# Order of the first loads, of one batch's transposes and of one PSUM bank in a fused attention and FFN kernel

## The chip, the cores and the metric

The kernel runs on one core of one Trainium2 chip. The metric is the time of one execution on the device, in microseconds; less is better.

## The reference

There are 8 batches, 12 heads, 448 tokens and 64 elements per head. First comes attention with a squared relu in place of softmax, then a normalized FFN with a residual:

```python
scores = (1 / sqrt(64)) * q @ k.T                  # (8, 12, 448, 448)
attn   = max(scores, 0)**2 / 448
x      = (attn @ v), heads side by side            # (8, 448, 768)
xn     = (x - mean(x)) / sqrt(var(x) + 1e-6) * g_ln
out    = x + max(xn @ w_ch1, 0) @ w_ch2            # w_ch1 768 x 3072, w_ch2 3072 x 768
```

Inputs and output are float32 in HBM. The kernel computes in bfloat16 with float32 sums.

## The kernel before

Two heads make a pair, so there are 6 pairs per batch and pairs are numbered on through the batches: pairs 0 to 5 are batch 0, 6 to 11 batch 1, pair 12 begins batch 2. All the program's engine queues are written out by hand: within `tc.manual_schedule` each engine executes its instructions in the order in which the Python code emits them. What an engine waits for is added by the framework from the tiles that an instruction reads and writes.

**Three kinds of DMA queue.** GpSimd (POOL) issues nearly all loads, since they cast float32 to bfloat16 on the way. SyncE (SP) issues the DMA transposes and the stores. ScalarE (ACT) issues one load at the start and half of the last stores. On each of POOL and SP a DMA also waits until the one that used its semaphore before, eight DMAs earlier, has landed.

**The start.** `load_heads` (lines 145 to 163) emits POOL's loads of q, k and v of batches 0 and 1 from a list of pieces, `(name, first head, number of heads)`. "k" loads the first 384 keys of each head and "k last" the other 64; "v last" is four small loads. `load_early` (190 to 202) brings heads 0 and 1, which are pair 0, on another way: q by SP and k by ACT, in float32 into space that is free at that time, and three casts on VectorE and ScalarE make them bfloat16. It also loads the gains `g_sb`. `make_identity` writes the 128 x 128 identity on POOL with a memset and an affine select; TensorE needs it for the transposes of q and k in batches 0 and 1 (`pe_T`, line 236).

Meanwhile TensorE runs 15 matmuls on zeros (`warm_up`, line 714). Then `att_T(0)` transposes pair 0, and `step_fine` (772) goes through pairs 0 to 5: QK (line 301, or 296 for the last 64 keys of two pairs), relu on ScalarE (311), square on VectorE (314), AV (331). `att_T(2)` comes within pair 1, `att_T(3)` and `att_T(4)` follow.

**Each batch** then has FFN1 (`ffn_1_all`) and FFN2. FFN1 makes 24 column tiles of h, one per `ni`, with 12 matmuls each (447) and a relu on ScalarE (449). At certain `ni` (`IN_SECOND` for batch 1: 3, 6, 9, 13, 15, 18, 21) an `excursion` puts in three QK pieces of the next batch's attention. When the last QK of a pair is emitted, `queued` emits the transpose of the pair three later, `att_T` at line 260, on SP, and the loads of the pair six later are put on a list for POOL. Pairs from 12 on are transposed by DMA from `qk_ring`, which has three places. Three tiles `qkT` hold the transposed pairs in turn, so pair 15's transpose waits until TensorE has read pair 12's.

**x in token order.** Attention leaves x transposed, in `xT`. `ffn_x(b, ki)` (line 424) is a DMA transpose on SP that puts one sixth of it into `x_tok`; it is read for the statistics (`ffn_stats`, three VectorE instructions, lines 438 to 440, at the `ni` of `STATS_AT`) and for the residual. In batch 1 all six are emitted in batch 0's FFN2 (`ffn_2_first`), ahead of pair 15's transpose, which is emitted at `ni` 6 of batch 1's FFN1.

**FFN2 of batches 1 to 7** (`ffn_2_all`, `seven`) works on pairs of token tiles, with seven products in place of eight. A product is 24 matmuls (522) into one of three PSUM banks c, d, a. There are four single banks: `f_turn.items` (here f0 and f1) and `spare` (f2 and f3). Batch 7's FFN1 ends with three `unit`s, which also make seven products (673) in place of eight, in all four banks. The last unit has c = spare[0], d = f1, a = f0 and e = spare[1]. Its bank c is read by lines 688 (ScalarE) and 689 (VectorE), its bank e by line 700. FFN2 of batch 7 then begins with a product in `z_bank`, which is spare[0]. The very last product is cut in two, 256 and 128 columns; the 128 columns go to spare[1].

Of the kernel before, what the change touches and what calls it, by code (L numbers as in the profile page):

```python
# [11 lines left out]
def kernel(  # L12
# [10 lines left out]
    nc = tc.nc  # L23
# [6 lines left out]
    B, H, S, D = q.shape  # L30
# [33 lines left out]
    ps_pool = ctx.enter_context(tc.tile_pool(name="ps", bufs=1, space=bass.MemoryType.PSUM))  # L64

    identity = const_pool.tile([P, P], bf16)
    make_identity(nc, identity)
    eps_sb = const_pool.tile([P, 1], fp32)
    nc.vector.memset(eps_sb, 1e-6)
    first_sqrt = const_pool.tile([P, 1], fp32)  # L70
# [462 lines left out]
    def seven(b, pair, banks, last, between):  # L533

        m1, m2 = 2 * pair, 2 * pair + 1
        a11, a12 = (h[:, r, h_cols(b, m1)] for r in (slice(0, KH), slice(KH, K2)))
        a21, a22 = (h[:, r, h_cols(b, m2)] for r in (slice(0, KH), slice(KH, K2)))
        c, d, a = (bk[:, :HD] for bk in banks)
        bb = c
        acc1, acc2 = new_acc(), new_acc()  # L540
        tt = nc.vector.tensor_tensor
        sums = {}

        def after3():
            nc.scalar.copy(acc1, c)

        def after4():
            tt(acc1, d, acc1, op=Alu.add)

        def after1():  # L550
            tt(acc2, a, acc1, op=Alu.add)

        def finish(o_t, y, m, dh):
            nc.scalar.activation(o_t, y, Act.Identity, scale=rstd[:, m:m + 1])  # L554
            nc.gpsimd.tensor_tensor(o_t, o_t, x_half(m, dh), op=Alu.add)  # L555
            store(o_t, m, dh * HD, (dh + 1) * HD)

        def after5():
            tt(acc1, acc1, c, op=Alu.subtract)  # L559
            finish(new_o(), c, m1, 1)  # L560
            before7()

        def after2():
            tt(acc2, acc2, d, op=Alu.subtract)
            if last:
                scaled_plus(acc2, acc2, m2, x_half(m2, 1))
            finish(new_o(), d, m2, 0)

        def before7():
            if last:  # L570
                scaled_plus(acc1, acc1, m1, x_half(m1, 0))

        def after7():
            if last:
                scaled_plus(acc1, a, m1, acc1)
                store(acc1, m1, 0, HD)
                return
            tt(acc1, a, acc1, op=Alu.add)
            finish(acc1, acc1, m1, 0)

        def after6():
            tt(acc2, bb, acc2, op=Alu.add)
            finish(acc2, acc2, m2, 1)

        def s(name, x, y, op):
            def run():
                sums[name] = sum_of(x, y, op)
            return run

        steps = [  # L590
            (lambda: product(c, a11, B12, True), s(1, a11, a22, Alu.add), after3),
            (lambda: product(d, a22, B21, True), s(5, a11, a12, Alu.add), after4),
            (lambda: product(a, sums[1], B_SUM, True), s(2, a21, a22, Alu.add), after1),
            (lambda: product(c, sums[5], B22, False), s(7, a12, a22, Alu.subtract), after5),
            (lambda: product(d, sums[2], B11, False), s(6, a21, a11, Alu.subtract), after2),
            (lambda: product(a, sums[7], B_BOT, False), None, after7),
        ]
        if not last:
            steps.append((lambda: product(bb, sums[6], B_TOP, True), None, after6))
        for n, (mm, pre, post) in enumerate(steps):  # L600
            mm()
            flush()
            if pre:
                pre()
            posts.append(post)
            between(n)
        if last:
            cut = HD - P
            parts = ((bb, 0, cut), (spare[1], cut, HD))
            for ps, d0, d1 in parts:  # L610
                product(ps, sums[6], B_TOP, True, d0, d1)
                flush()

                def after(ps=ps, d0=d0, d1=d1):
                    o_t = acc2[:, d0:d1]
                    scaled_plus(o_t, ps[:, :d1 - d0], m2, o_t)
                    store(o_t, m2, HD + d0, HD + d1, (nc.sync, nc.scalar))
                posts.append(after)
            flush()
# [227 lines left out]
    T_IN_FIRST = {10: 3, 13: 4, 16: 5}  # L847
    X_AT = (9, 10, 11, 12, 13, 14)
    V_AT = {22: PE_T * NPAIR + 2, 23: PE_T * NPAIR + 4}
    STATS_AT = {0: (18, 21, 23), 1: (10, 16, 19, 22), 2: (2, 5, 8, 14), 3: (2, 5, 8, 11)}  # L850
    IN_SECOND = (3, 6, 9, 13, 15, 18, 21)
    IN_REST = (1, 3, 6, 9, 12, 15, 18)
    X_SUMS_AT = {0: (0, 1, 2), 4: (3,), 7: (4,)}
# [1 line left out]
    def ffn_1_all(b):  # L855
        ms = tiles_of(b)
        units = () if b < UNIT_FROM else (UNIT,) if b < B - 1 else (*LAST_UNITS, UNIT)
        for ni in range(NI0 if b == 0 else 0, units[0] if units else K2):
            if b == 0 and ni == NI0:
                ffn_1_first()  # L860
            if b == 0 and ni == NI0 + 2:
                x_carry(0)
            if b == 0 and ni == X_AT[0]:

                nc.sync.dma_start(held, h[:1, ni - 1, CARRY:CARRY + 16])
            if b == 0 and ni in X_AT:
                ffn_x(b, X_AT.index(ni))
            if b == 0 and ni == IN_FIRST[-1] + 1:
                flush_loads()
            if b == 0 and ni in V_AT:  # L870
                load_v(V_AT[ni])
            bursts = (IN_FIRST, IN_SECOND, IN_REST)[min(b, 2)]

            late = ni == 0 and b > 1 and b * S // (2 * P) - (b - 1) * S // (2 * P) == 1
            ffn_1(ni, spare[1] if late or b < B - 1 and ni in bursts and len(ready) > 1 else None)
            flush()
            at = STATS_AT[min(b, 2) if b < B - 1 else 3][:len(ms)]
            if ni in at:
                ffn_stats(ms[at.index(ni)])
            if b >= UNIT_FROM:  # L880
                for n in X_SUMS_AT.get(ni, ()):
                    x_sum(n)
            if b == 1:
                for n, part in enumerate(p for p, at in zip(LATE_SUMS, SUMS_AT) if at == ni):
                    if ni == REST_AT and n < 2:
                        ffn_2_first_rest(n)
                    w2_sums(*part)
            if b == 0:
                if ni in IN_FIRST:
                    excursion(3)  # L890
                if ni == IN_FIRST[-1] + 3:
                    next_AV(bank=spare[1])
                if ni in T_IN_FIRST:
                    att_T(NPAIR + T_IN_FIRST[ni])
            elif b < B - 1:
                if ni in bursts:
                    first = nc.vector if b > 1 and ni == bursts[0] else nc.scalar
                    excursion(3, third=(first, nc.vector), **(dict(evac_by=nc.scalar) if b == 1 else {}))
                    while ni > bursts[1] and held_stores:
                        held_stores.pop(0)()  # L900
                if b == 1 and ni == K2 - 1:
                    flush_loads()
                    next_AV(bank=spare[1])

        late = []

        def between(n):
            if n == 2:
                flush_loads()
            if n == 3:  # L910
                next_AV(bank=sc_turn.items[0][:, 0], evac_by=nc.scalar, later=late)
            if n == 5:
                posts.extend(late)


        f0, f1 = f_turn.items
        if b == B - 1:
            unit(units[0], (f0, spare[1], spare[0], f1), accs[0], accs[2])
            unit(units[1], (f1, f0, spare[1], spare[0]), accs[3], accs[4])
            unit(units[2], (spare[0], f1, f0, spare[1]), accs[0], accs[2])  # L920
        elif units:
            unit(UNIT, (f0, spare[1], spare[0], f1), accs[0], accs[1], between)

    CENTER_AT = (4, 6, 8)

    REST_AT = 3
    SUMS_AT = (1, 2, 3, 3, 3, 4, 7, 11)
    LATE_SUMS = [(o, x, y, op, part)
                 for o, x, y, op in ((B_SUM, B11, B22, Alu.add), (B_BOT, B21, B22, Alu.add),
# [2 lines left out]
    def ffn_2_first():  # L932
        b = 0
# [5 lines left out]
        for dh in range(2):  # L939
            for m, part in [(m, part) for m in range(2) for part in range(2 if dh else 4)]:  # L940
# [5 lines left out]
                if n in CENTER_AT:  # L946
                    steps[CENTER_AT.index(n)]()
                if n == 2:
                    for ki in range(K1):
                        ffn_x(1, ki)  # L950
                if n == 8:
                    carry(b)
# [13 lines left out]
    def ffn_2_all(b):  # L966
# [2 lines left out]
        z_bank = spare[0]  # L969
        first = b * S // (2 * P)  # L970
        pairs = range(first, (b + 1) * S // (2 * P))
        banks = [z_bank, y_bank, x_bank] if b == B - 1 else [y_bank, z_bank, x_bank]
        todo = []
        if b < B - 1:
            assert not ready
# [27 lines left out]
    ENGINES = [E.PE, E.Pool, E.DVE, E.Activation, E.SP]  # L1003

    with tc.manual_schedule(engines=set(ENGINES)):
        load_heads(0, [("q", 2, 2), ("k", 2, 2), ("k last", 0, 4), ("q", 4, 4), ("k", 4, 4),
                       ("k last", 4, 4), ("v", 0, 4), ("v last", 0, H), ("q", 8, 4), ("k", 8, 4),
                       ("k last", 8, 4), ("v", 4, 4), ("v", 8, 4)])
        load_early()
        load_heads(1, [("q", 0, 2), ("k", 0, 2), ("k last", 0, H)])  # L1010
        load_heads(1, [("q", 2, 4), ("k", 2, 4)])
        load_w1(0)
# [58 lines left out]
```

## Time and profile before

| | |
|---|---|
| Median of 4 runs | 518.27 us (517.08 to 520.14) |
| The profiled execution | 517.88 us, span 516.0 us |
| TensorE matmuls | 509.6 us busy, 99% of the span |
| VectorE | 402.6 us, 78% |
| ScalarE | 287.5 us, 56% |
| POOL | 223.9 us, 43% |
| HBM | 51.91 MB read, 11.01 MB written |

The span goes from the first to the last instruction of the core. Times in the views are from its start, in us. "Landing" is the time at which the semaphore of a DMA has reached its full count; the DMA list gives it as time since the issue. Matmuls overlap, so a busy TensorE is not one at its peak, and the step from one matmul's start to the next one's tells more of a wait than the idle time does. In a timeline, brackets after a row give the engine's idle time before it and what ended it.

### The profile page before, as it was taken

The numbers are of one execution on the slowest core, as the hardware profiler recorded it, in microseconds if no ns is written. First come the engines' busy times: TensorE is split into PE (matmuls) and PEld (weight loads), VectorE is DVE, ScalarE is ACT, GpSimd is POOL, SyncE is SP. The second block draws the span as 40 slices with busy tenths as digits, with TensorE's granted clock in tenths as the row PEclk, the third lists the DMA queues.
The fourth block names the chain that finished last, engine by engine and source line by source line (L and its number), as shares of the span: only waits on it lengthen the run. The fifth ranks groups of instructions, "written<-read, shape, count | busy, mean of one in ns | idle before, by whom it ended". The sixth has DMA issues, their size and how long they took to land.

```text
span 516.0 us, 14345 instructions
## 1 busy us (share of the span) xinstructions
PE 509.6 (99%) x5974; PEld 325.5 (63%) x5974; DVE 402.6 (78%) x720; ACT 287.5 (56%) x487; POOL 223.9 (43%) x257
## 2 busy tenths in 40 slices
PE   8999999999999999999999999999999999999996
PEld 4445567547875576655766557655766557667986
DVE  4966779968988689687885869987896869993855
ACT  5986642786248762487624876487624875234220
POOL 9727114888433853237632385346632000330031
PEclk9999999999999999999999999999999999999999
DMA  9999999999537992479924799369925300240022
GB/s 134 185 198 201 182 204 164 145 194 124 79 80 115 116 93 63 108 85 121 97 61 105 76 135 133 72 81 110 95 65 107 63 1 3 72 114 1 3 61 64
DMA packets 175280, 53.05 MB, mean 103 GB/s; under 512 B 154224, under 2 KB 175216, under 8 KB 175216
## 3 DMA queue, kind: packets, MB, share of 16 engines
q0 software_dynamic: 103712, 25.75, 55.2%
q1 hardware_dynamic: 70976, 26.03, 27.4%
q8 instruction: 46, 0.75, 0.7%
q10 hardware_dynamic: 528, 0.37, 0.2%
q14 instruction: 18, 0.15, 0.1%
HBM read 51.91 MB, written 11.01 MB: 122 GB/s over the span
## 4 chain that ended last, share of the span: by engine, by line
PE 93%; DVE 3%; DMA 2%; ACT 1%; issue 0%
PE f L522 34%; PE f L447 34%; PE f L673 6%; PE f L331 5%; PE sc L301 4%; PE f L501 3%; PE f L301 2%; DMA qkT_t<-qk_ring 2%; DVE at L314 2%; PE sc L296 1%; ACT at L311 1%; PE f L354 1%; PE sc L331 1%; PE f L236 1%; PE f L836 1%; DMA h<-in_q_dram 1%
## 5 line engine op out<-in xcount | busy, mean ns | idle before, releaser
L447 PE MATMUL f<-xc,w 128*64 128x448 bf16 x1872 | 189.0, 354 | 0.1
L447 PEld LDWEIGHTS <-w 128*64 128x64 bf16 x1872 | 105.1, 110 | 76.8 <-issue 14.5
L522 PE MATMUL f<-w,s_sb 128*64 128x384 bf16 (+2 forms) x1584 | 130.1, 324 | 0.0
L449 ACT ACTIVATE h<-f 128x448 bf16<-128x448 f32 x156 | 85.9, 551 | 65.1 <-PE f L447 60.1
L522 PEld LDWEIGHTS <-s_sb 128*64 128x64 bf16 x1584 | 95.4, 110 | 31.8
L311 ACT ACTIVATE at<-sc 128x896 bf16<-128x896 f32 x120 | 102.9, 918 | 9.3 <-PE sc L301 9.0
L314 DVE TENSOR_TENSOR at<-at 128x896 bf16<-128x896 bf16 x168 | 96.3, 619 | 7.1 <-ACT at L311 6.2
L555 POOL TENSOR_TENSOR o_t<-o_t,x_tok 128x384 f32<-128x384 f32 x26 | 25.3, 972 | 153.2 <-ACT o_t L554 153.2
L175 POOL DMA_DIRECT2D qk_ring<-in_q_dram x36 | 47.2, 1312 | 81.0 <-DMA qkT_t<-qk_ring 56.6
L554 ACT ACTIVATE o_t<-f,rstd 128x384 f32<-128x384 f32 x26 | 15.1, 582 | 95.8 <-DVE acc_t L559 44.3
L516 DVE TENSOR_TENSOR s_sb<-h 128x1536 bf16<-128x1536 bf16 x65 | 64.3, 1004 | 0.0
L176 POOL DMA_DIRECT2D qk_ring<-in_k_dram x36 | 56.3, 1564 | 10.9 <-DMA w<-in_moe_w_ch_dram 10.9
L522 PE MATMUL f<-w,h 128*64 128x384 bf16 x624 | 53.0, 326 | 0.1
L177 POOL DMA_DIRECT2D qk_ring<-in_k_dram x36 | 47.5, 1320 | 4.8 <-DMA w<-in_moe_w_ch_dram 4.7
L307 DVE TENSOR_SCALAR at<-f 128x448 bf16<-128x448 f32 x59 | 35.6, 615 | 13.8 <-PE f L301 13.8
L522 PEld LDWEIGHTS <-h 128*64 128x64 bf16 x624 | 37.8, 110 | 12.6 <-issue 0.3
L555 POOL TENSOR_TENSOR acc_t<-acc_t,x_tok 128x384 f32<-128x384 f32 x24 | 28.5, 1196 | 20.0 <-ACT acc_t L554 16.9
L187 POOL DMA_DIRECT2D v_ring<-in_v_dram x36 | 33.5, 1220 | 0.4 <-DMA qk_ring<-in_q_dram 0.2
L411 DVE SCALAR_TENSOR_TENSOR xc<-f,g_sb,xc 128x448 bf16<-128x448 f32 x45 | 28.5, 678 | 4.2 <-PE f L405 4.2
L331 PE MATMUL f<-at,v_ring 128*64 128x448 bf16 x248 | 31.1, 357 | 0.0
L301 PE MATMUL sc<-qkT_t 64*128 64x448 bf16 x192 | 30.5, 362 | 0.0
L370 DVE TENSOR_SCALAR xT<-f 128x448 bf16<-128x448 f32 x22 | 13.6, 617 | 18.0 <-PE f L331 10.0
(130 smaller groups left out, 563.4 us busy)
## 6 DMA issues: line engine op xcount, KB each, us to landing
w<-in_moe_w_ch_dram POOLq DMA_DIRECT2D x6, 768.0 KB, 13.1
w<-in_moe_w_ch_dram POOLq DMA_DIRECT2D x4, 1152.0 KB, 28.8
v_ring<-in_v_dram POOLq DMA_DIRECT2D x21, 192.0 KB, 5.2
qk_ring<-in_q_dram POOLq DMA_DIRECT2D x36, 112.0 KB, 4.8
qk_ring<-in_k_dram POOLq DMA_DIRECT2D x36, 96.0 KB, 5.1
out_dram<-o_t SPq DMA_DIRECT2D x8, 168.0 KB, 2.2
out_dram<-acc_t SPq DMA_DIRECT2D x7, 168.0 KB, 2.4
out_dram<-o_t SPq DMA_DIRECT2D x8, 144.0 KB, 2.1
```

What stands on the lines that cost most here:

```text
L175: nc.gpsimd.dma_start(q_to, q[b, heads].rearrange("x (p j) d -> p j x d", j=NJ))
L176: nc.gpsimd.dma_start(k_to[:, :NF], k[b, heads, :SF].rearrange("x (p t) d -> p t x d", t=NF))
L177: nc.gpsimd.dma_start(k_to[:SS, NF], k[b, 2 * a:2 * a + 2, SF:].rearrange("x s d -> s x d"))
L301: nc.tensor.matmul(by_j(half[hh]), k_of(i, r, t, P), q_of(i, r), start=True, stop=True)
L311: nc.scalar.activation(at, ps[:, :, :S], Act.Relu)
L314: nc.vector.tensor_mul(attn[i, t], attn[i, t], attn[i, t])
L331: nc.tensor.matmul(ps[hh * D:(hh + 1) * D, :], weights, values, start=start, stop=stop)
L447: nc.tensor.matmul(ps[c * D:(c + 1) * D, :], w1[:, ki, n0:n0 + D], xc[:, ki, :], start=(ki == 0), stop=(ki == K1 - 1))
L449: nc.scalar.activation(h[:, ni, CARRY:], ps, Act.Relu)
L516: nc.vector.tensor_tensor(s_sb[:, n], x, y, op=op)
L522: nc.tensor.matmul(ps[c * D:(c + 1) * D, :d1 - d0], stat[:, ki, c * D:(c + 1) * D], w2[:, slot, ki, d0:d1], start=(start and ki == 0), sto ...
L555: nc.gpsimd.tensor_tensor(o_t, o_t, x_half(m, dh), op=Alu.add)
```

## The change

There are four parts.

1. `load_early` is emitted first, then POOL's loads of heads 2 and 3, then the identity. Emitting `load_early` first does not change the order on SP, ACT or VectorE. On POOL, memset and affine select now come behind two loads; before, they stood ahead of the first and of the second.
2. The loads of heads 4 to 7 (pairs 2 and 3) are split. Heads 4 and 5 keep their place, heads 6 and 7 come behind "v last". POOL issues two loads more.
3. Of batch 1's six x transposes three stay where they were, and three are emitted right after pair 15's transpose, at `ni` 6. The first statistics of batch 1 go from `ni` 10 to `ni` 14. On SP the order is three x, pair 15, three x, pair 16, where it was six x, pair 15, pair 16.
4. The banks of batch 7's FFN2 are spare[1], spare[0], f1 in place of spare[0], f1, f0. The last 128 columns go to f0 in place of spare[1].

```diff
     identity = const_pool.tile([P, P], bf16)
-    make_identity(nc, identity)
...
         if last:
             cut = HD - P
-            parts = ((bb, 0, cut), (spare[1], cut, HD))
+            parts = ((bb, 0, cut), (f_turn.items[0], cut, HD))
...
-    STATS_AT = {0: (18, 21, 23), 1: (10, 16, 19, 22), 2: (2, 5, 8, 14), 3: (2, 5, 8, 11)}
+    STATS_AT = {0: (18, 21, 23), 1: (14, 16, 19, 22), 2: (2, 5, 8, 14), 3: (2, 5, 8, 11)}
...
                     excursion(3, third=(first, nc.vector), **(dict(evac_by=nc.scalar) if b == 1 else {}))
+                    if b == 1 and ni == bursts[1]:
+                        for ki in range(X_FIRST, K1):
+                            ffn_x(1, ki)
...
+    X_FIRST = 3
...
                 if n == 2:
-                    for ki in range(K1):
+                    for ki in range(X_FIRST):
                         ffn_x(1, ki)
...
-        banks = [z_bank, y_bank, x_bank] if b == B - 1 else [y_bank, z_bank, x_bank]
+        banks = [spare[1], z_bank, y_bank] if b == B - 1 else [y_bank, z_bank, x_bank]
...
-        load_heads(0, [("q", 2, 2), ("k", 2, 2), ("k last", 0, 4), ("q", 4, 4), ("k", 4, 4),
-                       ("k last", 4, 4), ("v", 0, 4), ("v last", 0, H), ("q", 8, 4), ("k", 8, 4),
+        load_early()
+        load_heads(0, [("q", 2, 2), ("k", 2, 2)])
+        make_identity(nc, identity)
+        load_heads(0, [("k last", 0, 4), ("q", 4, 2), ("k", 4, 2), ("k last", 4, 4), ("v", 0, 4),
+                       ("v last", 0, H), ("q", 6, 2), ("k", 6, 2), ("q", 8, 4), ("k", 8, 4),
                        ("k last", 8, 4), ("v", 4, 4), ("v", 8, 4)])
-        load_early()
```

## The prediction

> **What bounds the kernel now.** I read the page first (busy shares and the chain of waits), then the waits of TensorE alone, then the timelines of the three places that the diff touches, and last the DMA list cut to one issue at a time, which gives each load's landing.
>
> ```profile
> PE 509.6 (99%) x5974; PEld 325.5 (63%) x5974; DVE 402.6 (78%) x720; ACT 287.5 (56%) x487; POOL 223.9 (43%) x257
> ...
> PE 93%; DVE 3%; DMA 2%; ACT 1%; issue 0%
> ```
>
> TensorE is busy for 509.6 of 516.0 us and carries 93% of the chain. A change that adds and removes no matmul can only move the few places where TensorE stands still. The waits of TensorE say how little they are:
>
> ```profile
> PE f L714 <- DVE w L109: 1.2, 1, 1.2
> PE f L236 <- DVE w L198: 0.3, 1, 0.3
> PE sc L296 <- DMA qkT_t<-qk_ring: 0.3, 1, 0.3
> PE f L236 <- DVE x_tok L370: 0.2, 1, 0.2
> ```
>
> The columns are total, times, longest, in us. Beyond these there are 4 us after the last matmul and pauses hidden in the modelled ends of matmuls: in the start times of single matmuls, 0.27 us before the key transposes at 5.49 (they should follow 0.05 us after the previous one and follow after 0.32), and 0.31 us before batch 7's FFN2 (below). So more than about 1 us of gain is not to be had; a loss has no such bound.
>
> **The start.** POOL issues its loads back to back; a load lands long after its issue:
>
> ```profile
> 0.74 0.20 POOL masks.py:197 MEMSET identity<- 128x128 bf16 x1 [0.29 <-POOLq L1055]
> 1.36 0.82 POOL L150 DMA_DIRECT2D w<-in_q_dram  x1 [0.41 <-issue]
> 2.27 0.31 POOL masks.py:199 TENSOR_SCALAR_AFFINE_SELECT identity<-identity 128x128 bf16<-128x128 bf16 x1
> 2.51 0.73 POOL L153 DMA_DIRECT2D w<-in_k_dram  x1
> ...
> 9.09 0.74 POOL L150 DMA_DIRECT2D w<-in_q_dram  x1
> 9.90 0.75 POOL L153 DMA_DIRECT2D w<-in_k_dram  x1
> 10.65 0.62 POOL L156 DMA_DIRECT2D w<-in_k_dram  x1
> 11.26 1.51 POOL L158 DMA_DIRECT2D v_ring<-in_v_dram  x2
> ```
>
> Pair 0 comes by SP (q, lands 4.36) and ACT (k, lands 5.06), issued at 0.75: already the first things on their queues, so calling load_early first moves nothing there. Only POOL's order changes. Landings before and first readers on TensorE: heads 2-3 at 5.74 and 5.96 (read 6.98); heads 4-7 at 8.54, 9.62, 9.85 (pair 2 read at 11.22, pair 3 at 13.74); v 0-3 with its last rows by 12.22 (12.94); heads 8-11 at 13.51, 14.61, 15.76 (16.86 to 17.4); v 4-7 at 16.99 (17.79). No load is waited for, so no load that comes earlier gains anything.
>
> (a) Heads 2-3 ahead of the identity. POOL's first load can leave at about 0.8 instead of 1.36, the second at 1.5 instead of 2.5; the identity is ready near 3.0 instead of 2.58, for a reader at 4.88: nothing. The gain is nothing, since 5.74 was early enough. The risk is pair 0's keys, for which TensorE does wait. The packets by queue in 3.25 to 3.75 us:
>
> ```profile
> q10 hardware_dynamic: 208, 0.16, 91.9%
> q1 hardware_dynamic: 93, 0.02, 18.3%
> ```
>
> q10 is ACT's queue with these keys, served at full rate; POOL's q0 shows its first packets only near 3.9, 2.5 us after its first issue, when the keys are nearly through. With the issue at 0.8 they come near 3.3. [...] Bounds 0 and 0.5; I take +0.25, on the path in full, as TensorE, ScalarE's cast and the rest follow in series.
>
> (b) Pair 2 alone. Of heads 4-7, heads 6-7 now follow v's last rows. Pair 2's loads are smaller by half and land about 1 us sooner, for a reader that has 1.4 us of slack: 0. But POOL issues two loads more, 2 x 0.75 = 1.5 us. Less 0.6 for the earlier start, plus up to 0.3 because memset and select stand in line now, everything from heads 8 on leaves POOL 0.9 to 1.3 us later; I take 1.2. Heads 6-7 leave at about 8.9 and 9.6; the same slot took 4.4 us for twice the bytes (9.09 to 13.51), so k lands near 13.6 for a reader at 14.1: 0. Heads 8's last keys 15.76 + 1.2 = 17.0 against 17.4: 0. v 4-7: 16.99 + 1.2 = 18.2 against 17.79 + 0.25 = 18.04: a new wait of +0.15 (0 to 0.5); queued behind it are QK of pair 3 and so ScalarE's relu. POOL's stream is then full until w2 is in (79.7), so its delay lasts: pair 12's transpose (issued 81.68, landed 87.67, read at 88.47) lands at 88.87 for a reader that is itself at 88.87 by now: 0 (up to 0.5).
>
> **Batch 1.**
>
> ```profile
> 87.72 7.92 SPq L424 DMA_TRANSPOSE x_tok<-xT  x6
> 95.83 5.96 SPq L260 DMA_TRANSPOSE qkT_t<-qk_ring  x2
> ...
> 104.22 0.38 PE L296 MATMUL sc<-qkT_t 64*64 64x448 bf16 x2 [0.28 <-DMA qkT_t<-qk_ring]
> ```
>
> Six x transposes stand ahead of pair 15's on SP, each 1.3 us to issue; pair 15's leaves at 95.83 and takes 8.3 us to land, at 104.18, and TensorE starts that matmul 0.62 us after the one before where 0.31 is usual. After the change three x transposes stand ahead. Pair 15's can leave once its own loads are in (the last landed at 95.16, about 1 us later by (b), a little sooner with less traffic) and TensorE has read pair 12's tile (93.2). Its landing then takes 5.5 to 6 us, as pair 17's did (107.02, 5.5) with a short queue: about 101.5. The wait goes: -0.32.
>
> What is moved back: the other three x transposes issue at about 97 to 101 and land near 104; pair 16's follows at 101 instead of 100.0 and lands near 107.2 instead of 106.52, for a reader near 108.5: 0. The eight stores behind it follow as before; the last of them shares pair 16's semaphore and left at 106.53, just as that landed, so pair 17's issue (107.02) hangs on pair 16's landing. Pair 17 landed at 112.53, read at 113.12: slack 0.6 against 0.7 of delay, with TensorE itself 0.1 late: 0 (0 to 0.6). POOL's loads for pair 18, which waited for pair 15's landing (104.75), start some 3 us sooner and mix with these transfers; that is inside the bound. VectorE's three statistics instructions (0.56 + 0.56 + 0.21 us) go from ni 10 to ni 14, behind the squares that end at 109.1; an idle stretch of 1.12 us at 112.6 takes them up, and the squares that wait for it are done by 112.7 for a reader at 113.8: 0.
>
> **Batch 7.** The matmul start times: the last unit's matmuls start 0.093 us after each other; FFN2's first starts 0.404 us after the last of them. The chain says why:
>
> ```profile
> 475.93 7.21 PE f L673 x150
> 483.14 0.02 issue
> 483.16 0.55 ACT h L688
> 483.72 0.02 issue
> 483.74 0.63 DVE s_sb L689
> 484.37 0.04 issue
> 484.42 27.54 PE f L522 x360
> ```
>
> Bank spare[0] is the unit's c, read by relu and then by the subtraction until 484.37. The new first bank, spare[1], is the unit's e, whose reader L700 ends at 483.58. The second product, now in spare[0], starts near 486.06. So -0.31, down to the end. The last quarter's bank, f0 instead of spare[1], has been idle since the unit: 0.
>
> **Sum** on this execution: 0.25 + 0.15 - 0.32 - 0.31 = -0.23. It took 517.88 (span 516.0 and 1.88 around it), so 517.65; the median of the runs is 0.39 above it: 518.04, say 518.0.
>
> **The rivals.**
> The late stream (slower). If POOL's stream is late by D, TensorE pays D - 1.05 at v 4-7 (slack 0.80 and the 0.25), and at pair 17 D - 0.6 less what TensorE is late itself. For: the loads of 10 to 14 us took 5 to 5.9 us to land, so their latency may grow with the issue. Against: part of D is made up where bytes, not issues, limit. It turns the sum from D = 1.4 on (0.25 + 0.35 - 0.63 is about 0); at D = 3 it gives 0.25 + 1.95 + 0.5 - 0.63 = +2.1, 520.4.
> The cold clock (slower). The 128x256 warm-up matmuls start 214 ns apart until 8.95 us and 109 ns apart at 9.97, so TensorE's clock came up near 9.7, though the granted clock reads 9 in all slices. [...]
> More gain (faster). If the median of 518.27 holds more waits for pair 2's or pair 15's data than the profiled execution, half of its distance to the fastest run (1.19) may go too: 518.27 - 0.63 - 0.6 = 517.0.
> It does nothing at the start: with (a) and (b) at 0, -0.63 gives 517.6.
>
> **How the numbers follow.** The sum as worked out with its bounds, or nothing at the start: 0.66. Late stream 0.14; cold clock 0.09; more gain 0.11. A difference under 0.5% (2.6 us: 515.7 to 520.9) is about what a measurement of this kernel cannot tell from none. Faster by more needs twice the pauses that exist: 0.05. Slower by more needs a late stream with D over 3.5 or both slow cases: 0.10. Within: 0.85. The range goes from 516.6 (more gain, and 0.4 for the spread of the runs) to 520.5 (late stream).
>
> **What would show it.** TensorE's waits without the line of pair 15; FFN2 of batch 7 starting 0.09 us after the unit; ScalarE's cast of the keys (5.08 before) near 5.3; POOL's load of v 4-7 issued near 12.5 and TensorE waiting for it near 18. Wrong would be: the keys not later, a wait over 1 us at pair 12 or 17, or a time outside the range.

## The result, and the profile after

The changed kernel takes 520.76 us in the median (517.75 to 524.5, 42 runs), the kernel before 518.57 us (63 runs beside them). The ratio is 1.0045, with a 95% interval of 1.0035 to 1.0056: 0.45% slower, which is within the 0.5% that the forecast called no change, and 0.26 us above the upper end of its range. The forecast was 518.0, a small gain; the measured difference is a loss of 2.3 us.

The profiled execution took 520.17 us with a span of 518.4, which is 2.29 more than the profiled execution before. The first page lines, in the order of those shown before:

```profile
PE 509.3 (98%) x5974; PEld 320.9 (62%) x5974; DVE 403.3 (78%) x720; ACT 287.7 (55%) x487; POOL 225.5 (44%) x259
...
PE 92%; DMA 2%; DVE 2%; POOL 2%; ACT 1%; issue 0%; POOLq 0%
```

TensorE is as busy as before and POOL has 2 instructions more, its two extra loads. POOL is now on the chain of waits with 2%, where it was not. The waits of TensorE (total, times, longest, in us; line numbers after the change are lower by one):

```profile
PE f L235 <- DMA w<-in_k_dram: 1.7, 1, 1.7
PE f L713 <- DVE w L108: 1.2, 1, 1.2
PE sc L295 <- DMA qkT_t<-qk_ring: 1.0, 1, 1.0
PE f L235 <- DVE w L197: 0.4, 1, 0.4
PE f L330 <- DMA v_ring<-in_v_dram: 0.2, 1, 0.2
```

Two of the larger ones are new: 1.7 us for keys in the start, and 1.0 us for pair 17's transpose (before, the same line stood there with 0.3 for pair 15's). To see what they cost I subtracted, matmul by matmul, the start times before from the start times after; both kernels issue the same 5974 matmuls in the same order.

| stretch | after minus before, us |
|---|---|
| end of the start, 22.5 (and up to batch 1) | +1.98 |
| from pair 15's matmuls in batch 1 (104.2 before) | +1.33 |
| from pair 17's matmuls in batch 1 (113.0 before) to the end of batch 7's FFN1 | +2.69 |
| first matmul of batch 7's FFN2 | +2.38 |
| last matmul | +2.35 |

So three places move: the start loses 1.98, batch 1 gains 0.64 at pair 15 and loses 1.35 at pair 17, and batch 7 gains 0.31. Nothing else moves by more than 0.03.

**The start.** TensorE's timeline after the change (start, busy us, what, and in brackets the idle time before and what ended it):

```profile
9.62 0.70 PE L235 MATMUL f<-identity,w 112*64 112x112 bf16 x16
...
12.13 0.36 PE L300 MATMUL sc<-qkT_t 64*128 64x448 bf16 x2
12.45 0.39 PE L235 MATMUL f<-identity,w 112*64 112x112 bf16 x8
14.54 0.67 PE L235 MATMUL f<-identity,w 128*64 128x128 bf16 x8 [1.70 <-DMA w<-in_k_dram]
15.14 0.55 PE L300 MATMUL sc<-qkT_t 64*128 64x448 bf16 x2
15.62 0.96 PE L330 MATMUL f<-at,v_ring 128*64 128x448 bf16 x4
...
18.26 0.36 PE L389 MATMUL f<-x_tok,ones 128*128 128x448 bf16 x1
```

and the same pieces before:

```profile
11.22 0.70 PE L236 MATMUL f<-identity,w 112*64 112x112 bf16 x16
...
13.74 0.70 PE L236 MATMUL f<-identity,w 112*64 112x112 bf16 x16
14.37 0.36 PE L301 MATMUL sc<-qkT_t 64*128 64x448 bf16 x2
14.66 0.57 PE L331 MATMUL f<-at,v_ring 128*64 128x448 bf16 x4
...
16.27 0.36 PE L390 MATMUL f<-x_tok,ones 128*128 128x448 bf16 x1
```

Three things are to be seen. First, TensorE arrives at pair 2 at 9.62 and not at 11.22, although no load made that possible: in this execution its full clock came at 4.40 us, in the execution before at 9.64 (14 transposes at 6.45 take 0.56 us here and 0.90 at 6.98 there; what set the moment is not shown). Second, pair 3's queries are transposed at 12.45, and then TensorE stands for its keys, whose load was issued at 9.89 and landed at 14.50; the page's chain has that load as one link. Third, after the wait the same two QK matmuls take 0.55 instead of 0.36. A view by stretches, with the granted clock as the third number from the end (behind it DMA share and GB/s), says why:

```profile
12.50:14.50 2.00, 0.34 (x8) 0.19 (x8) 0.90 (x2) 0.97 (x2) 2.00 (x4) 1.00 1.23 142
14.50:18.30 3.80, 3.76 (x25) 1.12 (x25) 2.08 (x4) 1.83 (x2) 3.80 (x6) 0.55 1.55 175
```

The clock was at half from 14.64 to 18.05 (mean granted clock 0.50 over that stretch). From the QK behind the transposes to the row of line 389 it is 18.26 - 15.14 = 3.12 us, before 16.27 - 14.37 = 1.90: +1.22, and the eight key transposes ahead of it took 0.60 for half of 0.63: +0.28. So half clock costs 1.5 us. The account of the start: TensorE comes to pair 3 earlier by 1.29, waits 1.7, and pays 1.5 for the clock: +1.9, of 1.98.

**POOL's first loads** did not come earlier:

```profile
1.32 0.83 POOL L149 DMA_DIRECT2D w<-in_q_dram  x1 [0.86 <-POOLq L1061]
2.13 0.73 POOL L152 DMA_DIRECT2D w<-in_k_dram  x1
2.86 0.23 POOL masks.py:197 MEMSET identity<- 128x128 bf16 x1
3.16 0.29 POOL masks.py:199 TENSOR_SCALAR_AFFINE_SELECT identity<-identity 128x128 bf16<-128x128 bf16 x1
3.40 0.62 POOL L155 DMA_DIRECT2D w<-in_k_dram  x1
```

The first left at 1.32 (1.36 before) with nothing in front of it, and the third at 3.40 (3.23 before), since memset and select stand ahead of it now. Pair 0's keys landed at 5.04 (5.06) and ScalarE's cast of them began at 5.07 (5.08). The packets by queue in 3.25 to 3.75 us, with q10 the one of these keys and q0 POOL's (packets, MB, share of 16 engines):

```profile
q10 hardware_dynamic: 180, 0.13, 77.0%
q1 hardware_dynamic: 256, 0.02, 36.2%
q0 software_dynamic: 2, 0.00, 1.5%
```

POOL's queue has two packets among them.

**Batch 1.** SP's timeline, of which the rows from 87.72 on before the change stand in the prediction. There pair 17's transpose left with the group

```profile
107.02 14.14 SPq L260 DMA_TRANSPOSE qkT_t<-qk_ring  x4
```

and after the change:

```profile
97.22 1.23 SPq L259 DMA_TRANSPOSE qkT_t<-qk_ring  x1
98.51 4.06 SPq L423 DMA_TRANSPOSE x_tok<-xT  x3
102.75 1.61 SPq L259 DMA_TRANSPOSE qkT_t<-qk_ring  x1
104.45 2.01 SPq L474 DMA_DIRECT2D out_dram<-o_t  x4
106.55 2.81 SPq L474 DMA_DIRECT2D out_dram<-acc_t  x4
109.64 9.05 SPq L259 DMA_TRANSPOSE qkT_t<-qk_ring  x3
```

Pair 15's transpose lands at 102.51, and TensorE no longer waits for it. But pair 16's leaves at 102.75 instead of 100.00 and lands at 109.03 (106.52). The eight stores follow, and the last, which shares pair 16's semaphore, leaves at 109.05, just after that landing. So pair 17's leaves at 109.64 (107.02) and lands at 115.58 (112.53). The matmuls that read it are two of a group of four that started together before:

```profile
112.95 0.36 PE L296 MATMUL sc<-qkT_t 64*64 64x448 bf16 x4
```

and now stand apart:

```profile
114.29 0.35 PE L295 MATMUL sc<-qkT_t 64*64 64x448 bf16 x2
115.62 0.38 PE L295 MATMUL sc<-qkT_t 64*64 64x448 bf16 x2 [0.98 <-DMA qkT_t<-qk_ring]
```

That is the loss of 1.35. At pair 15 it is the other way round: the group was split by 0.62 before (103.60 and 104.22) and starts together now, at 105.58.

**Batch 7.** The chain of waits goes from the last unit to FFN2 with no ScalarE and VectorE between:

```profile
474.88 12.07 PE f L672 x252
486.96 27.35 PE f L521 x360
```

### The profile page after: what moved, and what is told of

Same layout as the page of the kernel before. It is cut to its first block, busy times and chain, and to the rows that moved or that the text cites. A ratio compares the mean times of both kernels' runs of the same rounds, so it can differ in the third digit from the quotient of the medians.

```text
span 518.4 us, 14350 instructions
## 1 busy us (share of the span) xinstructions
PE 509.3 (98%) x5974; PEld 320.9 (62%) x5974; DVE 403.3 (78%) x720; ACT 287.7 (55%) x487; POOL 225.5 (44%) x259
## 4 chain that ended last, share of the span: by engine, by line
PE 92%; DMA 2%; DVE 2%; POOL 2%; ACT 1%; issue 0%; POOLq 0%
PE f L521 34%; PE f L446 34%; PE f L672 6%; PE f L330 5%; PE sc L300 4%; PE f L500 3%; PE f L300 2%; DMA qkT_t<-qk_ring 1%; PE sc L295 1%; DVE at L313 1%; DMA w<-in_k_dram 1%; ACT at L310 1%; PE f L353 1%; PE sc L330 1%; PE f L835 1%; POOL v_ring L161 0%
## 5 line engine op out<-in xcount | busy, mean ns | idle before, releaser
L521 PEld LDWEIGHTS <-s_sb 128*64 128x64 bf16 x1584 | 92.4, 110 | 34.8
L175 POOL DMA_DIRECT2D qk_ring<-in_k_dram x36 | 55.6, 1543 | 12.0 <-DMA w<-in_moe_w_ch_dram 12.0
L176 POOL DMA_DIRECT2D qk_ring<-in_k_dram x36 | 46.5, 1292 | 5.2 <-DMA w<-in_moe_w_ch_dram 4.9
L521 PEld LDWEIGHTS <-h 128*64 128x64 bf16 x624 | 36.5, 110 | 13.5
L369 DVE TENSOR_SCALAR xT<-f 128x448 bf16<-128x448 f32 x22 | 13.6, 617 | 20.2 <-ACT at L310 11.1
```

Source lines behind the costliest of these rows:

```text
L175: nc.gpsimd.dma_start(k_to[:, :NF], k[b, heads, :SF].rearrange("x (p t) d -> p t x d", t=NF))
L176: nc.gpsimd.dma_start(k_to[:SS, NF], k[b, 2 * a:2 * a + 2, SF:].rearrange("x s d -> s x d"))
L521: nc.tensor.matmul(ps[c * D:(c + 1) * D, :d1 - d0], stat[:, ki, c * D:(c + 1) * D], w2[:, slot, ki, d0:d1], start=(start and ki == 0), sto ...
```

## The experiments

All ratios are to the kernel before, measured on the same chip beside it, with 95% intervals. "Half-clock runs" counts the executions whose mean granted clock reads 0.997 or less: one stretch of 3.41 us at half rate, as in the trace above, makes 1 - 3.41 / 2 / 518 = 0.9967. (The clock also falls behind the last matmuls. Of that at most 2.0 us lie within the span in the 17 traces, and alone they read 0.998. So the count is a sign of such stretches and no proof.) Of the changed kernel 25 of 43 executions are of that kind, with a median of 521.24 us; the 18 others have 520.10, which is still 1.5 above the kernel before.

**Each part alone, and the whole without one part**

The whole with heads 4 to 7 loaded as before (parts 1, 3 and 4):

```diff
-        load_heads(0, [("k last", 0, 4), ("q", 4, 2), ("k", 4, 2), ("k last", 4, 4), ("v", 0, 4),
-                       ("v last", 0, H), ("q", 6, 2), ("k", 6, 2), ("q", 8, 4), ("k", 8, 4),
+        load_heads(0, [("k last", 0, 4), ("q", 4, 4), ("k", 4, 4), ("k last", 4, 4), ("v", 0, 4),
+                       ("v last", 0, H), ("q", 8, 4), ("k", 8, 4),
```

> The changed kernel with heads 4 to 7 loaded whole again (parts 1, 3 and 4 stay). Theory A (pair 3's keys, put behind v's last rows, are the loss: TensorE waits about 2 us for them, and the wait brings 3.4 us at half clock after it): TensorE has no wait at pair 3's transposes, no half clock between 14 and 18 us, and the time falls by about 1.8 us from the changed kernel's 520.8 to 519.0 (+0.1% against before). Theory B (the regrouped x transposes are the loss, by the 1.0 us wait at pair 17): no fall, 520.5. Theory C (POOL's first loads ahead of the identity slow pair 0's keys): no fall either, and the cast of the keys starts later than 5.08.

Measured: 1.0011 (0.9996 to 1.0026), 3 half-clock runs of 22. Most of the loss goes with the split. In its profile pair 3 waits for nothing, but pair 17 does, for 3.0 us, since its transpose leaves at 109.32 behind the stores and lands at 116.48. So the loss in batch 1 does not need the split, nor a TensorE that is late: at 22.5 us it is 0.26 earlier here than before.

The whole with the x transposes in one group, as before (parts 1, 2 and 4):

```diff
-    STATS_AT = {0: (18, 21, 23), 1: (14, 16, 19, 22), 2: (2, 5, 8, 14), 3: (2, 5, 8, 11)}
+    STATS_AT = {0: (18, 21, 23), 1: (10, 16, 19, 22), 2: (2, 5, 8, 14), 3: (2, 5, 8, 11)}
...
-    X_FIRST = 3
+    X_FIRST = K1
```

> The changed kernel with batch 1's six x transposes in one group ahead of pair 15's again, first statistics at ni 10 (parts 1, 2 and 4 stay). Theory A: still about +1.5 us against before, 520.1, with the wait for pair 3's keys; the wait at pair 17 (1.0 us) goes and the one at pair 15 (0.3 us) comes back, so 0.7 less than the changed kernel. Theory B: back to before or a little under it, 518.2 to 518.6.

Measured: 1.0023 (1.0012 to 1.0034), 15 half-clock runs of 22. Pair 17 does not wait; the start still loses 3.13 us in the profiled execution, with 1.9 of waiting for pair 3's queries, then 0.6 and 0.5 for pair 4's keys and v, and a half-clock stretch behind these two, from 19.5 to 22.9 (granted 0.57 over 19 to 23).

The split alone, on the kernel before (part 2):

```diff
-        load_heads(0, [("q", 2, 2), ("k", 2, 2), ("k last", 0, 4), ("q", 4, 4), ("k", 4, 4),
-                       ("k last", 4, 4), ("v", 0, 4), ("v last", 0, H), ("q", 8, 4), ("k", 8, 4),
+        load_heads(0, [("q", 2, 2), ("k", 2, 2), ("k last", 0, 4), ("q", 4, 2), ("k", 4, 2),
+                       ("k last", 4, 4), ("v", 0, 4), ("v last", 0, H), ("q", 6, 2), ("k", 6, 2), ("q", 8, 4), ("k", 8, 4),
```

> The kernel before with only the split: heads 6 and 7 behind v's last rows. Theory A: +1.8 us against before (520.4, +0.35%), the wait for pair 3's keys in the trace, and half clock after it in most executions. Theories B and C: no difference, within 0.2%.

Measured: 1.0032 (1.0021 to 1.0043), 519.56 us, 10 half-clock runs of 22. Its timeline of TensorE repeats what the changed kernel shows, here at the queries:

```profile
13.64 0.95 PE L236 MATMUL f<-identity,w 112*64 112x112 bf16 x16 [1.55 <-DMA w<-in_q_dram]
14.53 0.55 PE L301 MATMUL sc<-qkT_t 64*128 64x448 bf16 x2
```

The wait, and then QK at 0.55: half clock, from 14.16 to 17.57 (granted 0.53 over 14.0 to 17.6). But the ten half-clock runs are no slower than the twelve others (medians 519.59 and 519.48; the kernel before has 518.05 at full clock). By this sign the split loses 1.4 us in executions without such a stretch as well.

The bank alone (part 4):

```diff
-            parts = ((bb, 0, cut), (spare[1], cut, HD))
+            parts = ((bb, 0, cut), (f_turn.items[0], cut, HD))
...
-        banks = [z_bank, y_bank, x_bank] if b == B - 1 else [y_bank, z_bank, x_bank]
+        banks = [spare[1], z_bank, y_bank] if b == B - 1 else [y_bank, z_bank, x_bank]
```

> The kernel before with only the other banks in batch 7's FFN2. All theories: -0.3 us (-0.06%), at the edge of what the times resolve; in the trace the first product of batch 7's FFN2 starts 0.09 us after the last unit's last matmul instead of 0.40. A rival: the wait moves to the second product, which now takes the bank that is free at 484.37; then the later product starts late and nothing is gained.

Measured: 0.9986 (0.9978 to 0.9993), no half-clock run of 22. A gain of 0.36 to 1.14 us; the trace has 0.31 of it at batch 7. Its waits tell more, because up to batch 7 this kernel is the kernel before:

```profile
PE sc L301 <- DMA qkT_t<-qk_ring: 1.2, 1, 1.2
PE f L236 <- DMA w<-in_k_dram: 0.7, 1, 0.7
PE sc L296 <- DMA qkT_t<-qk_ring: 0.5, 1, 0.5
PE f L331 <- DMA v_ring<-in_v_dram: 0.4, 1, 0.4
```

In an execution whose full clock comes at 5.59, the loads of before are late too: pair 2's last keys, v, pair 12 and pair 17 are all waited for. The execution that the prediction was read from had none of these waits.

The two groups of x transposes alone (part 3):

> The kernel before with only the x transposes in two groups (and the first statistics at ni 14). From the runs so far (changed kernel +0.45%, without this part +0.23%) it should cost about 1.0 us: 519.2, +0.2%. Theory A (queue order): pair 15's wait goes, pair 17's comes, of 1 to 3 us, since pair 17's transpose stands on SP behind pair 16's and eight stores, the last of which waits for pair 16's landing. Theory B (the moved statistics hold VectorE and through it TensorE): no wait on a transpose at pair 17, instead waits on VectorE between 105 and 117 us.

The edit is that of `STATS_AT`, `X_FIRST` and `ffn_x` in the change's diff. Measured: 1.0032 (1.0014 to 1.0050), 8 half-clock runs of 17. It loses alone, without the two extra loads:

```profile
PE sc L296 <- DMA qkT_t<-qk_ring: 0.8, 1, 0.8
PE sc L301 <- DMA qkT_t<-qk_ring: 0.5, 1, 0.5
```

The first is pair 17 (issued 108.37, landed 113.58), the second pair 12. Its profiled execution is only 0.6 us above that of before and has no half-clock stretch; in batch 1 it loses 1.09 at pair 17 and gains 0.62 at pair 15. The nine executions at full clock agree with that: 518.54, against 518.09 for the kernel before at full clock. Most of the loss lies in the eight half-clock runs, with a median of 521.51. That is 3.4 us, twice the 1.7 that one stretch of 3.41 us at half rate can cost, and no trace shows such an execution.

The identity behind the first loads alone (part 1):

> The kernel before with only the order on POOL: heads 2 and 3 ahead of the identity. Theory A (POOL's first load starts at 1.32 whatever stands ahead of it, and memset and select then come between the second and the third load): every load from the third on is about 0.2 us later, pair 0's keys land at 5.05 as before; the time is between 0 and +0.25 us of before, 518.1 to 518.4. Theory B (the loads now meet pair 0's keys on the DMA engines): keys land 0.25 us later, +0.25 us or more.

The edit is the two moved lines and the load list cut after `("k", 2, 2)`. Measured: 0.9999 (0.9987 to 1.0011), 2 half-clock runs of 14: nothing. Its profiled execution is one of the two; TensorE waits 1.1 us for v, and half clock follows from 19.3 to 22.7 (the four AV matmuls take 0.57 at 18.26 and 0.96 at 19.34).

The four parts alone sum to -0.0001 + 0.0032 + 0.0032 - 0.0014 = 0.0049, and the whole is 0.0045. So the parts add, and two of them lose.

**Why the split loses: its place, or its two issues?**

The whole with heads 6 and 7 loaded right behind 4 and 5, ahead of v:

```diff
-        load_heads(0, [("k last", 0, 4), ("q", 4, 2), ("k", 4, 2), ("k last", 4, 4), ("v", 0, 4),
-                       ("v last", 0, H), ("q", 6, 2), ("k", 6, 2), ("q", 8, 4), ("k", 8, 4),
+        load_heads(0, [("k last", 0, 4), ("q", 4, 2), ("k", 4, 2), ("q", 6, 2), ("k", 6, 2), ("k last", 4, 4), ("v", 0, 4),
+                       ("v last", 0, H), ("q", 8, 4), ("k", 8, 4),
```

> The changed kernel with heads 6 and 7's q and k right behind heads 4 and 5's, ahead of v (still loads of their own). Theory A (their place behind v is the loss): no wait for pair 3's keys and no half clock after it; v 0-3 lands about 1.3 us later and its first reader waits up to 1.3 us. Between the changed kernel without the split (+0.11%) and the changed kernel (+0.45%): about 519.3, +0.25%. Theory B (the two issues more on POOL are the loss, wherever they stand): no better than the changed kernel, 520.5.

Measured: 1.0042 (1.0022 to 1.0063), 8 half-clock runs of 12. Pair 3 waits for nothing, and the ratio is that of the change within the intervals. TensorE's timeline has the waits at other readers:

```profile
10.60 0.22 PE L235 MATMUL f<-identity,w 64*64 64x64 bf16 x2 [0.78 <-DMA w<-in_k_dram]
...
12.09 0.57 PE L330 MATMUL f<-at,v_ring 128*64 128x448 bf16 x4 [0.98 <-DMA v_ring<-in_v_dram]
```

This kernel still had the groups in it, so the same was done to the kernel before alone:

```diff
-        load_heads(0, [("q", 2, 2), ("k", 2, 2), ("k last", 0, 4), ("q", 4, 4), ("k", 4, 4),
+        load_heads(0, [("q", 2, 2), ("k", 2, 2), ("k last", 0, 4), ("q", 4, 2), ("k", 4, 2), ("q", 6, 2), ("k", 6, 2),
```

> Before, with the loads of heads 4 to 7 split into q 4-5, k 4-5, q 6-7, k 6-7, all ahead of the last keys and of v: two more issues, none of them behind v. Place theory (the split costs because pair 3's loads stand behind v 0-3): no wait for pair 3, at most +0.1% against before (518.7 or less). Count theory (two more issues push everything behind them back by 1.2 to 1.4 us wherever they stand): v 0-3 and v 4-7 land 1 us later, the waits for v or pair 12 grow by about 1 us, ratio 1.002 to 1.004 (519.2 to 520.3), as for the split alone (1.0032).

Measured: 1.0027 (1.0017 to 1.0037), 519.47 us, 6 half-clock runs of 16. This is the count of issues, not the place: v 0-3 is issued at 7.22 (5.89 before), v 4-7 at 12.55 (11.26), and TensorE waits for both:

```profile
11.66 0.57 PE L331 MATMUL f<-at,v_ring 128*64 128x448 bf16 x4 [0.90 <-DMA v_ring<-in_v_dram]
...
18.73 0.57 PE L331 MATMUL f<-at,v_ring 128*64 128x448 bf16 x4 [1.05 <-DMA v_ring<-in_v_dram]
```

The place only decides which reader waits.

**Why the groups lose: the stores ahead of pair 17**

Part 3 alone, with the stores held back from `ni` 9 to `ni` 15, behind pair 17's transpose:

```diff
-                    while ni > bursts[1] and held_stores:
+                    if b == 1 and ni == bursts[1]:
+                        for ki in range(X_FIRST, K1):
+                            ffn_x(1, ki)
+                    while ni > bursts[3] and held_stores:
```

> The kernel before with the x transposes in two groups and the held stores of batch 0 released four bursts later, from ni 15, behind pair 17's and 18's transposes on SP. Theory A (queue order): pair 17's transpose leaves near 107 instead of 109.6 and its wait is gone or under 0.3 us; with pair 15's wait gone as well the time falls below before by up to 0.5 us: 517.7. Theory B (VectorE): as the x groups alone, +0.2%. Theory C (bytes: the transposes and loads of that stretch fill the DMA engines, whatever their order): the wait at pair 17 stays over 0.7 us.

Measured: 0.9976 (0.9966 to 0.9985), 516.93 us, 1 half-clock run of 22. Against part 3 as it stands, measured beside it (1.0032), that is 2.6 us. SP's timeline:

```profile
96.73 4.02 SPq L424 DMA_TRANSPOSE x_tok<-xT  x3
100.94 8.84 SPq L260 DMA_TRANSPOSE qkT_t<-qk_ring  x3
109.87 2.03 SPq L475 DMA_DIRECT2D out_dram<-o_t  x4
```

Pairs 16, 17 and 18 leave together; pair 17's goes at 104.19 instead of 108.37 and lands at 108.95, and between 80 and 125 us TensorE waits for no data. In the later batches the stores are later too, and the start times there do not move. With the bank as well (the edits of part 3, of the stores and of part 4):

> The kernel before with the x transposes in two groups, the stores released later, and the other banks in batch 7's FFN2. If the measured parts add up (-0.24% and -0.14%): 516.3, -0.38%. A rival: they don't add, because the bank alone was measured better (-0.7 us) than the 0.31 us that its wait holds; then -0.30%.

Measured: 0.9974 (0.9962 to 0.9985), 517.1 us. The bank adds nothing that these intervals could show. Do the later stores alone do it? The same kernel with the six x transposes in one group:

> As the one before, but with the six x transposes in one group (first statistics at ni 10): only the stores go later, and the banks change. Theory A1 (both steps of the SP order count: pair 15 behind six transposes, pair 17 behind eight stores): pair 15's wait of about 0.3 us stays, pair 17's is gone: 0.3 us above the other, 516.6. Theory A2 (the stores were all of it; the two groups bring nothing): equal. Theory A3 (the gain comes from the groups, and the later stores only take back what they cost): near the bank alone, -0.14%, 517.5.

Measured: 0.9987 (0.9972 to 1.0001), 517.77 us. TensorE waits 1.6 us for pair 15, which leaves at 98.71 behind six x transposes and lands at 105.25. So in the traces the groups do what they are for, once the stores do not stand ahead of pair 17. The times do not show it: the step between the two kernels, 0.0013, is inside their intervals.

**One issue fewer at the start**

If two issues more cost 1.6 us, one fewer should gain. "k last" of heads 0 to 7 in one load, otherwise the kernel before:

```diff
-        load_heads(0, [("q", 2, 2), ("k", 2, 2), ("k last", 0, 4), ("q", 4, 4), ("k", 4, 4),
-                       ("k last", 4, 4), ("v", 0, 4), ("v last", 0, H), ("q", 8, 4), ("k", 8, 4),
+        load_heads(0, [("q", 2, 2), ("k", 2, 2), ("k last", 0, 8), ("q", 4, 4), ("k", 4, 4),
+                       ("v", 0, 4), ("v last", 0, H), ("q", 8, 4), ("k", 8, 4),
```

> The kernel before with one load less on POOL at the start: the last 64 keys of heads 0 to 7 in one load, where there were two. The split's opposite. Theory A (every issue on POOL makes all that follow later by its 0.65 us, and TensorE waits for v and heads 8 to 11 in most executions): v 0-3, v 4-7 and the stream behind them land 0.4 to 0.6 us sooner, the waits at v shrink by that; -0.3 to -0.5 us, 517.8. Theory B (bytes, not issues, limit the start): landings as before within 0.2 us, and no difference.

Measured: 1.0006 (0.9991 to 1.0021), no gain. In its profiled execution the start ends 1.14 us earlier than in the one before, and then one wait takes more than that back:

```profile
PE sc L301 <- DMA qkT_t<-qk_ring: 1.8, 1, 1.8
```

It is pair 12 at 89.17. Its transpose was issued at 81.65 and landed at 89.12. TensorE was early and the transpose was not: it was issued at the same time as before (81.68) and landed 1.45 later than before (87.67). Nor is the early start sure. In three more traces with the merged load (below) the start ends 0.74, 0.41 and 0.03 earlier than in the profile before, and in five with the loads of before 0.09 to 0.53 earlier.

The merged load with the groups, the later stores and the bank:

> Two groups of x transposes, stores later, the other banks, and the last keys of heads 0 to 7 in one load. If the parts add up: 0.3 to 0.5 us under the kernel without the merged load, 515.9, -0.45%. Rival: no better, since pair 12's transpose then takes the wait (its loads end with the weight stream, whose bytes are the same).

Measured: 0.9972 (0.9961 to 0.9984), 517.03 us; its profiled span is 514.6. Against the same without the merged load (0.9974): nothing.

Does pair 12 hold the gain back? Its loads ahead of the last weights:

```diff
-        load_w2(B22, 1, 1)
         nc.gpsimd.memset(qk_ring, 0.0)
         i = PE_T * NPAIR
         load_qk(i)
+        load_w2(B22, 1, 1)
```

> The groups with later stores, the bank and the merged last keys, and now pair 12's two loads stand ahead of the last w2 load in POOL's queue. Theory (pair 12's transpose hangs on the end of the weight stream and takes back what the start gains): no wait at pair 12 at all, 0.5 to 0.8 us below the same kernel without the move, near 516.3, ratio to before 0.9955 to 0.9965. Rival (the last w2 rows are late instead and their reader waits): the step moves to FFN2's first reader of those rows, ratio 0.997 to 0.998 as without the move.

> Before, with the last keys of heads 0 to 7 in one load and pair 12's two loads ahead of the last w2 load. Gate theory: the merged load starts FFN1 about 1 us earlier (27.8 against 28.9) and pair 12, no longer behind the whole stream, does not take it back: 0.5 to 1 us below before, ratio 0.998 to 0.999. Rival (the gain of the start is swallowed by other waits too, v or pair 17): ratio 1.000 to 1.001 as for the merged load alone.

Measured: 0.9969 (0.9958 to 0.9981; six runs, 516.6 us) with all the rest, and 0.9993 (0.9982 to 1.0004) with the merged load alone. The wait at pair 12 is gone in both traces (with all the rest its transpose lands at 84.70). The time moves by -0.0003 and -0.0013 against the same kernels without the move; both are inside the intervals. In the second kernel two small waits stand in its place, 0.3 at the first matmuls of batch 1's FFN1 and 0.5 at pair 17. Whether it costs anything that pair 12's loads stand behind the weights is not settled.

## Why the prediction was wrong

By its own steps, with the part's ratio times 518 us as the measured size:

| step | forecast, us | measured, us |
|---|---|---|
| (a) heads 2-3 ahead of the identity | +0.25 | 0.0 (-0.7 to +0.6) |
| (b) pair 2 alone | +0.15 | +1.7 (1.1 to 2.2) |
| batch 1 | -0.32 | +1.7 (0.7 to 2.6) |
| batch 7 | -0.31 | -0.7 (-1.1 to -0.4) |

(a) was wrong in its mechanism, though its price was small. POOL's first load does not leave at 0.8 when the identity is taken away from in front of it, but at 1.32. Its first packets came at 3.67 and only two were there by 3.75, beside 180 of the keys' queue, so the two queues hardly met up to then; the keys landed at 5.04 (5.06 before). The +0.25 was the author's estimate, and a delay of that kind was not shown.

(b) is the step that failed first: "k lands near 13.6 for a reader at 14.1: 0", and with it "No load is waited for". Both sides were off. The keys landed at 14.50, 0.9 later (they left 0.3 later and were 4.61 us under way, not 4.0), and the reader was ready at 12.84, the end of the query transposes. The reader's times had been taken from an execution whose full clock came at 9.64. The prediction had read that late clock, but priced only a further loss of it and not that readers come earlier without it. In the other sixteen traces of this study it came between 3.90 and 7.03, and TensorE is then 1.3 to 2.0 us earlier at pair 2. Five of these traces have the loads of before (the bank alone, the x groups alone, and the three with later stores and no merged load). In them the slack is gone; here the x groups with later stores:

```profile
11.12 0.57 PE L331 MATMUL f<-at,v_ring 128*64 128x448 bf16 x4 [0.57 <-DMA v_ring<-in_v_dram]
...
17.70 0.57 PE L331 MATMUL f<-at,v_ring 128*64 128x448 bf16 x4 [0.54 <-DMA v_ring<-in_v_dram]
```

By 22.5 us these five have only 0.1 to 0.5 us left of their lead; waits for loads have taken the rest. So the slack of 0.80 at v 4-7, from which the late-stream rival counted, was the slack of one unusual execution. The delay of POOL's stream was forecast well (1.2; v 4-7 was issued 1.40 later than in the profile before, and 0.6 to 1.3 later than in the five). With no slack ahead of it, such a delay is paid in full: the split alone loses 1.4 us in its executions at full clock, and the split ahead of v 1.6, at other readers.

The late stream was thus the right rival with its turning point in the wrong place: the prediction let it decide from D = 1.4, where its sum was about 0. And the cold clock, which had a chance of 0.09 and, as the author's estimate, a price of 1.7 us, came in, but behind a wait at 13 us and not in the warm-up: 1.5 us in the profiled execution, and 1.1 between the half-clock runs of the changed kernel and the others. The prediction had them as two rare cases on their own; in the kernels with the split they come together (64 half-clock runs of 115, the change itself counted, against 9 of 172 in ten others). What the half clock adds to the loss is not settled, since in the split alone it adds nothing that the times show.

Batch 1: "slack 0.6 against 0.7 of delay" was mis-sized, on both sides. Two readings were off, since the four matmuls of such a group start together and not 0.31 apart: pair 15's wait was worth 0.64 and not 0.32, and pair 17 was read at 112.96 and not at 113.12, which leaves a slack of 0.43. Pair 15's wait did go, for the reason given. But pair 16's transpose left 2.75 later than before, where the forecast had 1. The three x transposes took the 4 us that the forecast gave them. What came later was pair 15's own, at 97.22: its loads landed 1.91 later (97.07) and not about 1, as POOL issues them once pair 12's transpose has landed, which was 2.0 later (89.67). So part of the late stream of (b) comes back here. In the trace of the groups with later stores, where the start is that of before, pair 16's transpose leaves 0.94 later, as forecast. In the changed kernel pair 17's landing was 3.05 later. Its slack took up 0.43 of that and the delay of TensorE by then 1.33; the rest is 1.29, against a measured loss of 1.35. The order of the queue had been read correctly down to the shared semaphore.

Batch 7 was right: FFN2 follows the unit without the pause, 0.09 behind its last matmul. The bank alone gained somewhat more than 0.31; its interval ends at 0.36, and where the rest would lie no trace shows.

Two smaller slips: 1.5 - 0.6 with 0 to 0.3 added is 0.9 to 1.2, not 1.3; and "more than about 1 us of gain is not to be had" held for the execution that was read, not for the kernel, since the groups with later stores gain 0.8 to 1.8 us.

What stays open: why the groups alone have half-clock runs in 8 of 17, and why these lose 3.4 us. The profiled execution is not one of them. With the stores behind pair 17 they are rare (1 of 22). But they are rare as well with heads 4 to 7 whole (3 of 22), where batch 1 is as in the change, so the groups do not bring them alone.

## What to carry to other kernels

Read slack from more than one execution, or ask what set the reader's time: where a clock comes up at a varying moment (here between 3.90 and 9.64 us), a profile in which nothing waits may only be one in which the readers came late. On a queue that is full from end to end, count every issue added as a delay of all that follows (here two issues of 0.7 us made v 4-7 leave 1.40 later), and price it at whichever reader has least slack; where the new load stands only chose that reader here. The reverse was not shown: one issue fewer gained nothing. And when a transfer is brought forward in a queue, follow the last thing that is pushed back, here pair 17 behind eight stores: moving those stores was worth more than the move itself.

## What the runs showed of the hardware

- Half clock for 3.41 us came into the start of four traces: the changed kernel (14.64 to 18.05), the split alone (14.16 to 17.57), the x transposes in one group (19.5 to 22.9), the identity alone (19.3 to 22.7). Shortly ahead of it TensorE had waited for loads for 1.7, 1.55, 1.1 (0.6 and 0.5) and 1.3 us (0.3 and 1.1). The length of the waits does not decide alone: 1.9 us at pair 3 (x transposes in one group, up to 13.96; granted clock 1.00 from 14.0 to 17.6), 1.6 us at pair 15 (six x in one group, stores later; mean clock 0.999) and 3.0 us at pair 17 (heads 4 to 7 whole; 0.998) left the clock at full. What does decide was not shown.
- The mean granted clock of each timed execution is a sign of such stretches without a trace. The four kernels with the split (10 of 22, 15 of 22, 8 of 12, 6 of 16) and the groups alone (8 of 17) have them in about half of their runs, as has the change; the other ten kernels in 9 of 172 runs together, and the kernel before in 12 of 217.
- POOL's first DMA left at 1.32 to 1.36 us in all 17 traces, whether the identity's memset stood ahead of it or not.
- Half the bytes did not mean half the time on POOL's queue in the start. Issued near 9.9 us, keys of 96 KB took 4.61 us from issue to landing, and keys of 192 KB before 4.71; issued near 4.6 us, they took 3.80 and 5.08. The issue itself took POOL 0.7 to 0.8 us in all four cases.
